# Two chained products behind a convolution: paired 64-row passes, larger units, and a DMA transpose

## The chip, the cores and the metric

One NeuronCore of a Trainium2 chip runs the whole program. The metric is the device time of one execution in microseconds (us), lower is better. The kernel before takes 1038.2 us, the median of 3 runs (1037.63 to 1038.45).

Engines in the text: PE is TensorE (matmuls; PEld is its weight load), DVE is VectorE, ACT is ScalarE, POOL is GpSimd, and SP is SyncE, which here only issues DMAs. Matmuls read SBUF and write PSUM, which has eight banks of 2 KB per partition.

## The reference

Input x has 8 sequences of 4096 tokens with 192 channels. The 192 channels are 8 heads of 24. Each head has 7 weights, put through a softmax; every channel is convolved causally along its sequence with the weights of its head. Then come two products with a product with the cosine between them:

```python
# attention part: x (8, 4096, 192), weight (8, 7)
w = softmax(weight, axis=-1)
x_pad = concatenate([zeros((B, 6, D)), x], axis=1)          # causal
out[b, s, h, g] = sum_k w[h, k] * x_pad[b, s + k, h, g]
# then, on 32768 tokens x 192 channels:
h = x @ w_in            # 192 -> 2048
g = h * np.cos(h)
return g @ w_out        # 2048 -> 192, float32
```

## The kernel before, in words

The tokens are cut into 64 tiles of 512. Constants first: two sets of eight 128x128 band matrices (`band`, lines 93 to 105, and `bandhi`, lines 107 to 121) are put together tap by tap on DVE and POOL from shifted identities and the softmax weights. One matmul with such a matrix convolves 128 tokens; `bandhi` brings in the six tokens that lie across the block's edge. The two weight matrices are loaded in float32 and turned to bf16 on ACT (lines 127 to 133).

For each tile:

- `prep_tile` loads 512 tokens, 128 per block, on SP's queue (line 157), turns them to bf16 on POOL (line 160), and loads the last six tokens of the tile by themselves (`hx`, lines 162 to 166).
- `conv_tile` runs, for each of 4 blocks and 8 heads, two matmuls of 24 columns into `ct_ps` (lines 180 and 182): 64 in a tile. The result, tokens on partitions, goes to `ct_sb` in bf16 (lines 185 and 187). Eight PE transposes (line 191) turn it to channels on partitions, in two halves of 96 channels, and two copies put it into `convT`.
- Product 1 (line 207): for each of 16 blocks of 128 features, two matmuls of 96 rows and 512 columns into one bank, `h_ps` (three buffers).
- ACT computes the cosine as a sine with a shift of pi/2 (line 210), 128x512 at a time, and DVE multiplies `h_ps` by it into `g_sb` (line 211).
- Product 2 (line 224): for each of 4 token blocks, 16 matmuls of 192 columns add up in `o_ps` (one bank), which DVE copies to `o_sb` (line 226). SP stores the tile (line 227).

The order of the instructions on each engine is chosen by the framework's scheduler from the dependencies and the program order. In the trace it mixes the product 2 of a tile with the product 1 of the next, and the convolution of the tile after in small pieces between them.

Of the kernel before, what the change touches and what calls it, by code (L numbers as in the profile page):

```python
# [12 lines left out]
ALU = mybir.AluOpType  # L14


@with_exitstack
def kernel(
# [32 lines left out]
    nc.vector.tensor_reduce(out=wmax, in_=w_sb, axis=mybir.AxisListType.X, op=ALU.max)
# [8 lines left out]
    wsm = consts.tile([H, K], BF16)  # L60
    nc.vector.tensor_scalar(out=wsm, in0=wexp, scalar1=winv, scalar2=None, op0=ALU.mult)
    cidx = consts.tile([H, H * K], FP32)
    nc.gpsimd.iota(cidx, pattern=[[1, H * K]], base=0, channel_multiplier=0, allow_small_or_imprecise_dtypes=True)
    hidx = consts.tile([H, 1], FP32)
    nc.gpsimd.iota(hidx, pattern=[[0, 1]], base=0, channel_multiplier=K, allow_small_or_imprecise_dtypes=True)
    tdiff = consts.tile([H, H * K], FP32)
    nc.vector.tensor_scalar(out=tdiff, in0=cidx, scalar1=hidx, scalar2=None, op0=ALU.subtract)
    ge0 = consts.tile([H, H * K], FP32)
    nc.vector.tensor_scalar(out=ge0, in0=tdiff, scalar1=-0.5, scalar2=None, op0=ALU.is_gt)
    ltK = consts.tile([H, H * K], FP32)  # L70
    nc.vector.tensor_scalar(out=ltK, in0=tdiff, scalar1=float(K) - 0.5, scalar2=None, op0=ALU.is_lt)
    hm = consts.tile([H, H * K], FP32)
    nc.vector.tensor_tensor(out=hm, in0=ge0, in1=ltK, op=ALU.mult)
    wsm_rep = consts.tile([H, H, K], FP32)
    for hh in range(H):
        nc.scalar.copy(wsm_rep[:, hh, :], wsm)
    wsm_exp = consts.tile([H, H * K], BF16)
    nc.vector.tensor_tensor(out=wsm_exp, in0=hm, in1=wsm_rep.rearrange("p a b -> p (a b)"), op=ALU.mult)
    ones8 = consts.tile([H, 128], BF16)
    nc.vector.memset(ones8, 1.0)  # L80
    wb_ps = xtp.tile([128, H * K], FP32)
    nc.tensor.matmul(out=wb_ps, lhsT=ones8, rhs=wsm_exp, start=True, stop=True)
    wb = consts.tile([128, H * K], FP32)
    nc.scalar.copy(wb, wb_ps)
# [4 lines left out]
    identx = consts.tile([128, 128 + K], BF16)  # L89
    nc.vector.memset(identx, 0.0)  # L90
    nc.gpsimd.tensor_copy(out=identx[:, 0:128], in_=ident)

    band = consts.tile([128, H, 128], BF16)
    bacc = consts.tile([128, 2, 128], FP32)
    btmp = consts.tile([128, 2, 128], FP32)
    eng = [nc.vector, nc.gpsimd]
    for h in range(H):
        b = bacc[:, h % 2, :]
        tmp = btmp[:, h % 2, :]
        nc.vector.tensor_scalar(out=b, in0=identx[:, 0:128], scalar1=wb[:, h * K : h * K + 1], scalar2=None, op0=ALU.mult)  # L100
        for k in range(1, K):
            e = eng[k % 2]
            e.tensor_scalar(out=tmp, in0=identx[:, k : k + 128], scalar1=wb[:, h * K + k : h * K + k + 1], scalar2=None, op0=ALU.mult)  # L103
            nc.vector.tensor_tensor(out=b, in0=b, in1=tmp, op=ALU.add)  # L104
        nc.scalar.copy(band[:, h, :], b)  # L105

    bandhi = consts.tile([128, H, 128], BF16)
    dmat = consts.tile([128, 128], FP32)
    nc.gpsimd.iota(dmat, pattern=[[1, 128]], base=0, channel_multiplier=-1, allow_small_or_imprecise_dtypes=True)
    mc = consts.tile([128, K - 1, 128], FP32)  # L110
    for ci in range(K - 1):
        nc.vector.tensor_scalar(out=mc[:, ci, :], in0=dmat, scalar1=float(122 + ci), scalar2=None, op0=ALU.is_equal)
    for h in range(H):
        b = bacc[:, h % 2, :]
        tmp = btmp[:, h % 2, :]
        nc.vector.tensor_scalar(out=b, in0=mc[:, 0, :], scalar1=wb[:, h * K + 6 : h * K + 7], scalar2=None, op0=ALU.mult)
        for ci in range(1, K - 1):
            e = eng[ci % 2]
            e.tensor_scalar(out=tmp, in0=mc[:, ci, :], scalar1=wb[:, h * K + 6 - ci : h * K + 7 - ci], scalar2=None, op0=ALU.mult)  # L119
            nc.vector.tensor_tensor(out=b, in0=b, in1=tmp, op=ALU.add)  # L120
        nc.scalar.copy(bandhi[:, h, :], b)  # L121

    w_in_f32 = consts.tile([HD, 2, Dff], FP32)
    for c in range(2):
        nc.sync.dma_start(out=w_in_f32[:, c, :], in_=moe_w_in[c * HD : (c + 1) * HD, :])
    w_in_sb = consts.tile([HD, 2, Dff], BF16)
    nc.scalar.copy(w_in_sb[:, 0, :], w_in_f32[:, 0, :])
    nc.scalar.copy(w_in_sb[:, 1, :], w_in_f32[:, 1, :])

    w_out_f32 = consts.tile([128, NF, D], FP32)  # L130
    nc.sync.dma_start(out=w_out_f32, in_=moe_w_out.rearrange("(n p) d -> p n d", p=128))
    w_out_sb = consts.tile([128, NF, D], BF16)
    nc.scalar.copy(w_out_sb, w_out_f32)


    xin = ctx.enter_context(tc.tile_pool(name="xin", bufs=3))
    xbf_pool = ctx.enter_context(tc.tile_pool(name="xbf", bufs=2))
    hx_pool = ctx.enter_context(tc.tile_pool(name="hx", bufs=2))
    ct_pool = ctx.enter_context(tc.tile_pool(name="ct", bufs=2))
    convT_pool = ctx.enter_context(tc.tile_pool(name="convT", bufs=2))  # L140
    cos_pool = ctx.enter_context(tc.tile_pool(name="cos", bufs=3))
    gpool = ctx.enter_context(tc.tile_pool(name="g", bufs=2))
    opool = ctx.enter_context(tc.tile_pool(name="o", bufs=3))
    ct_ps_pool = ctx.enter_context(tc.tile_pool(name="ct_ps", bufs=2, space=bass.MemoryType.PSUM))
    h_ps_pool = ctx.enter_context(tc.tile_pool(name="h_ps", bufs=3, space=bass.MemoryType.PSUM))
    o_ps_pool = ctx.enter_context(tc.tile_pool(name="o_ps", bufs=1, space=bass.MemoryType.PSUM))

    def prep_tile(it):
        t0 = it * T
        x_f32 = xin.tile([128, 4, D], FP32)  # L150
        if it % TPB == 0:
            nc.vector.memset(x_f32[0:PAD, 0, :], 0.0)
            nc.sync.dma_start(out=x_f32[PAD:128, 0, :], in_=xf[t0 : t0 + 128 - PAD, :])
            nc.sync.dma_start(out=x_f32[:, 1:4, :],
                              in_=xf[t0 + 128 - PAD : t0 + T - PAD, :].rearrange("(n p) d -> p n d", p=128))
        else:
            nc.sync.dma_start(out=x_f32, in_=xf[t0 - PAD : t0 + T - PAD, :].rearrange("(n p) d -> p n d", p=128))
        x_bf = xbf_pool.tile([128, 4, D], BF16)
        for s in range(4):
            nc.gpsimd.tensor_copy(out=x_bf[:, s, :], in_=x_f32[:, s, :])  # L160
        hx = hx_pool.tile([128, 2, D], FP32)
        nc.sync.dma_start(out=hx[0 : PAD, 0, :], in_=xf[t0 + T - PAD : t0 + T, :])
        nc.gpsimd.memset(hx[:, 1, :], 0.0)
        nc.gpsimd.tensor_copy(out=hx[0:PAD, 1, :], in_=hx[0:PAD, 0, :])  # L164
        hx_bf = hx_pool.tile([128, D], BF16)
        nc.gpsimd.tensor_copy(out=hx_bf, in_=hx[:, 1, :])  # L166
        state["x_bf"] = x_bf
        state["hx_bf"] = hx_bf

    def conv_tile():  # L170
        x_bf = state["x_bf"]
        convT = convT_pool.tile([HD, 2, T], BF16)
        ct_sb = ct_pool.tile([128, 4, D], BF16)
        for sp in range(2):
            ct_ps = ct_ps_pool.tile([128, 2, D], FP32)
            for s2 in range(2):
                s = sp * 2 + s2
                nxt = x_bf[:, s + 1, :] if s < 3 else state["hx_bf"]
                for h in range(H):
                    nc.tensor.matmul(out=ct_ps[:, s2, h * G : (h + 1) * G], lhsT=band[:, h, :],  # L180
# [8 lines left out]
        for c in range(2):  # L189
            for s in range(4):  # L190
                nc.tensor.transpose(ps_t[:, c, s, :], ct_sb[:, s, c * HD : (c + 1) * HD], ident)  # L191
# [66 lines left out]
```

## Time and profile before

| what | value |
|---|---|
| median of 3 runs | 1038.2 us (1037.63 to 1038.45) |
| span of the profiled execution, first to last instruction | 1036.6 us |
| PE busy | 960.7 us (93%) |
| DVE busy | 831.1 us (80%) |
| ACT busy | 724.4 us (70%) |
| POOL busy | 166.8 us (16%) |
| DMA moved | 55.45 MB |

The span is that of one profiled execution; the median of the timed runs lies 1.6 us above it. Busy times overlap across engines, so the engine with the largest busy time isn't by that alone the bound: the chain of work that ended last tells that. A matmul's row lasts from its start to its modelled end, and the next matmul starts before that end, so the time from start to start is what a matmul costs in a row of many. The granted TensorE clock is full speed in this profile.

### The profile page before, as it was taken

The numbers are of one execution on the slowest core, as the hardware profiler recorded it, in microseconds if no ns is written. First come the engines' busy times: TensorE is split into PE (matmuls) and PEld (weight loads), VectorE is DVE, ScalarE is ACT, GpSimd is POOL, SyncE is SP. The second block draws the span as 40 slices with busy tenths as digits, with TensorE's granted clock in tenths as the row PEclk, the third lists the DMA queues.
The fourth block names the chain that finished last, engine by engine and source line by source line (L and its number), as shares of the span: only waits on it lengthen the run. The fifth ranks groups of instructions, "written<-read, shape, count | busy, mean of one in ns | idle before, by whom it ended". The sixth has DMA issues, their size and how long they took to land.

```text
span 1036.6 us, 26549 instructions
## 1 busy us (share of the span) xinstructions
PE 960.7 (93%) x10753; PEld 681.3 (66%) x10753; DVE 831.1 (80%) x1643; ACT 724.4 (70%) x1247; POOL 166.8 (16%) x506
## 2 busy tenths in 40 slices
PE   0039999999999999999999999999999999999997
PEld 0026677777777776777677677767776776777664
DVE  3658888888888888888788888888888888888885
ACT  3028777777777777777777777777677777777874
POOL 4651101110111111111101110111111011111100
PEclk9999999999999999999999999999999999999999
DMA  6001112211221122112111211121112112111010
GB/s 181 17 16 47 54 42 62 63 48 48 62 63 47 48 63 58 52 48 62 51 59 48 62 59 51 48 63 47 52 58 63 48 48 63 58 52 32 32 33 31
DMA packets 70748, 55.45 MB, mean 53 GB/s; under 512 B 2512, under 2 KB 70432, under 8 KB 70432
## 3 DMA queue, kind: packets, MB, share of 16 engines
q1 hardware_dynamic: 70624, 53.75, 17.2%
q8 instruction: 84, 1.38, 0.6%
q14 instruction: 40, 0.33, 0.1%
HBM read 28.57 MB, written 25.17 MB: 52 GB/s over the span
## 4 chain that ended last, share of the span: by engine, by line
PE 91%; POOL 3%; DVE 2%; ACT 1%; DMA 1%; issue 1%; SPq 0%; POOLq 0%
PE h_ps L207 44%; PE o_ps L224 34%; PE ct_ps L182 5%; PE ct_ps L180 5%; PE ps_t L191 4%; POOL btmp L119 1%; POOL btmp L103 1%; DMA w_in_f<-in_moe_w_in_dram 1%; DVE bacc L104 1%; ACT convT L192 0%; DVE bacc L120 0%; ACT cos_sb L210 0%; DVE btmp L103 0%; DVE g_sb L211 0%; DVE btmp L119 0%
## 5 line engine op out<-in xcount | busy, mean ns | idle before, releaser
L210 ACT ACTIVATE cos_sb<-h_ps,halfpi 128x512 bf16<-128x512 f32 x1024 | 660.4, 686 | 243.5 <-PE h_ps L207 222.1
L211 DVE TENSOR_TENSOR g_sb<-h_ps,cos_sb 128x512 bf16<-128x512 f32 x1024 | 667.8, 687 | 141.3 <-ACT cos_sb L210 131.2
L207 PE MATMUL h_ps<-convT,w_in_sb 96*128 96x512 bf16 x2048 | 579.1, 380 | 2.4 <-DVE g_sb L211 0.4
L224 PE MATMUL o_ps<-w_out_sb,g_sb 128*128 128x192 bf16 x4096 | 461.7, 246 | 2.6 <-DVE o_sb L226 1.3
L224 PEld LDWEIGHTS <-g_sb 128*128 128x128 bf16 x4096 | 352.1, 98 | 107.4 <-issue 18.1
L207 PEld LDWEIGHTS <-w_in_sb 96*128 96x128 bf16 x2048 | 185.6, 98 | 63.1 <-issue 5.4
L182 PEld LDWEIGHTS <-bandhi 128*128 128x128 bf16 x2048 | 126.0, 96 | 82.1 <-ACT bandhi L121 47.3
L160 POOL CAST x_bf<-x_f 128x192 bf16<-128x192 f32 x256 | 78.0, 343 | 597.2 <-PE ct_ps L182 597.2
L180 PEld LDWEIGHTS <-band 128*128 128x128 bf16 x2048 | 132.0, 96 | 54.8 <-ACT band L105 19.0
L180 PE MATMUL ct_ps<-x_bf,band 128*128 128x24 bf16 x2048 | 149.5, 174 | 16.2 <-ACT band L105 14.4
L182 PE MATMUL ct_ps<-x_bf,bandhi 128*128 128x24 bf16 x1536 | 116.8, 173 | 45.0 <-ACT bandhi L121 45.0
L226 DVE COPY o_sb<-o_ps 128x192 f32<-128x192 f32 x256 | 90.0, 352 | 24.3 <-PE o_ps L224 22.5
L191 PEld LDWEIGHTS <-ct_sb 128*96 128x96 bf16 x512 | 53.8, 123 | 42.4 <-ACT ct_sb L187 22.9
L191 PE MATMUL ps_t<-ident,ct_sb 128*96 128x128 bf16 x512 | 81.1, 231 | 0.1
L164 POOL COPY hx<-hx 6x192 f32<-6x192 f32 x64 | 21.4, 334 | 180.6 <-DMA hx<-in_x_dram 180.6
L185 DVE CAST ct_sb<-ct_ps 128x192 bf16<-128x192 f32 x128 | 43.5, 348 | 4.5 <-PE ct_ps L182 4.4
L187 ACT CAST ct_sb<-ct_ps 128x192 bf16<-128x192 f32 x128 | 40.5, 318 | 1.4 <-PE ct_ps L182 1.3
L192 ACT COPY convT<-ps_t 96x512 bf16<-96x512 bf16 x64 | 36.5, 570 | 1.0 <-PE ps_t L191 1.0
L182 PE MATMUL ct_ps<-hx_bf,bandhi 128*128 128x24 bf16 x512 | 36.0, 173 | 0.0
L193 DVE COPY convT<-ps_t 96x512 bf16<-96x512 bf16 x64 | 26.2, 410 | 0.0
L104 DVE TENSOR_TENSOR bacc<-bacc,btmp 128x128 f32<-128x128 f32 x48 | 13.4, 300 | 11.8 <-POOL btmp L103 11.6
L166 POOL CAST hx_bf<-hx 128x192 bf16<-128x192 f32 x64 | 22.0, 343 | 0.1
(45 smaller groups left out, 95.1 us busy)
## 6 DMA issues: line engine op xcount, KB each, us to landing
out_dram<-o_sb SPq DMA_DIRECT2D x64, 384.0 KB
x_f<-in_x_dram SPq DMA_DIRECT2D x56, 384.0 KB
x_f<-in_x_dram SPq DMA_DIRECT2D x8, 288.0 KB
w_in_f<-in_moe_w_in_dram SPq DMA_DIRECT2D x2, 768.0 KB
w_out_f<-in_moe_w_out_dram SPq DMA_DIRECT2D x1, 1536.0 KB
hx<-in_x_dram SPq DMA_DIRECT2D x64, 4.5 KB
x_f<-in_x_dram SPq DMA_DIRECT2D x8, 91.5 KB
w_sb<-in_weight_dram SPq DMA_DIRECT2D x1, 0.2 KB
```

What stands on the lines that cost most here:

```text
L160: nc.gpsimd.tensor_copy(out=x_bf[:, s, :], in_=x_f32[:, s, :])
L180: nc.tensor.matmul(out=ct_ps[:, s2, h * G : (h + 1) * G], lhsT=band[:, h, :], rhs=x_bf[:, s, h * G : (h + 1) * G], start=True, stop=False)
L182: nc.tensor.matmul(out=ct_ps[:, s2, h * G : (h + 1) * G], lhsT=bandhi[:, h, :], rhs=nxt[:, h * G : (h + 1) * G], start=False, stop=True)
L185: nc.vector.tensor_copy(out=ct_sb[:, s, :], in_=ct_ps[:, s2, :])
L187: nc.scalar.copy(ct_sb[:, s, :], ct_ps[:, s2, :])
L191: nc.tensor.transpose(ps_t[:, c, s, :], ct_sb[:, s, c * HD : (c + 1) * HD], ident)
L192: nc.scalar.copy(convT[:, 0, :], ps_t[:, 0, :, :])
L207: nc.tensor.matmul(out=h_ps, lhsT=w_in_sb[:, c, f * 128 : (f + 1) * 128], rhs=conv_sb[:, c, :], start=(c == 0), stop=(c == 1))
L210: nc.scalar.activation(out=cos_sb, in_=h_ps, func=AF.Sin, bias=halfpi, scale=1.0)
L211: nc.vector.tensor_tensor(out=g_sb[:, f, :], in0=h_ps, in1=cos_sb, op=ALU.mult)
L224: nc.tensor.matmul(out=o_ps[:, s2, 0:D], lhsT=g_sb[:, f, s * 128 : (s + 1) * 128], rhs=w_out_sb[:, f, :], start=(f == 0), stop=(f == NF - 1))
L226: nc.vector.tensor_copy(out=o_sb[:, s, :], in_=o_ps[:, s2, 0:D])
```

## The change

The kernel is written anew, with the same result. The parts:

- The order on each engine is now that of the program (`manual_schedule`).
- Product 1 splits the 192 channels as 128 + 64 instead of 96 + 96. Two blocks of features (`i` = 0, 1) are handled together: two 64-row matmuls, the first on partitions 0 to 63 and the second on 64 to 127, then two 128-row ones. The last 64 channels therefore stand twice in the transposed data.
- Sine and product take both blocks at once, 128x1024 over two banks; `h` has three buffers of two banks.
- The convolution works on units of 1024 tokens: for each head two matmuls of 8 x 24 = 192 columns; one ACT copy for two heads. The six tokens across an edge come from the block before (`xb[:, 0:UB]`), so no small load is needed.
- The transposes are one crossbar DMA for a unit, on SP's queue, behind a POOL copy that doubles the last 64 channels.
- The output copy is on ACT, two token blocks (one bank) at a time.
- The band matrices come from one row for each head, stored to DRAM, read back with a shift of one element per partition, and reversed on DVE.
- Loads are 1024 tokens, weight casts are on DVE and POOL.

The core of the diff (the lines removed are those of the functions above):

```diff
+    skew = consts.tile([128, H, 256], BF16)
+    nc.scalar.dma_start(out=skew, in_=bass.AP(tensor=rd.tensor, offset=rd.offset, ap=[[1, 128], [LR, H], [1, 256]]))
+    band = consts.tile([128, H, 256], BF16)
+    nc.vector.tensor_copy(out=band, in_=skew[:, :, ::-1])
...
+    def cast_unit(u):
...
+            nc.gpsimd.tensor_copy(out=xb[:, 0, :], in_=bf[u - 1][:, UB, :])
+        nc.gpsimd.tensor_copy(out=xb[:, 1 : UB + 1, :], in_=xt)
...
+    def conv_pair(u, q):
...
+        ps = c_pool.tile([128, 2, UB, G], FP32, name="c_ps")
+        for i in range(2):
+            h = 2 * q + i
+            hs = slice(h * G, (h + 1) * G)
+            nc.tensor.matmul(out=ps[:, i], lhsT=band[:, h, 0:128], rhs=xb[:, 1 : UB + 1, hs], start=True, stop=False)
+            nc.tensor.matmul(out=ps[:, i], lhsT=band[:, h, 128:256], rhs=xb[:, 0:UB, hs], start=False, stop=True)
...
+    def conv_out(q, ct, ps):
+        o = ct[:, :, 2 * q * G : (2 * q + 2) * G].rearrange("p n (i g) -> p i n g", i=2)
+        nc.scalar.copy(o, ps)
...
+    def turn_unit(u):
+        ct = ct_tiles.pop(u)
+        nc.gpsimd.tensor_copy(out=ct[:, :, D:256], in_=ct[:, :, 128:D])
+        t = cT_pool.tile([128, UB, 2, 128], BF16, name="cT")
+        nc.sync.dma_start_transpose(out=t.rearrange("p n c k -> p (n c) k"), in_=ct.rearrange("p n k -> p (n k)"))
...
+    def mm1(t, j):
...
+        h = h_pool.tile([128, 2, T], FP32, name="h")
+        for i in range(2):
+            r = slice(64 * i, 64 * i + 64)
+            nc.tensor.matmul(out=h[:, i, :], lhsT=w2[r, j, :], rhs=c[r, n0 : n0 + NB, 1, :], start=True, stop=False)
+        for i in range(2):
+            f = 2 * j + i
+            nc.tensor.matmul(out=h[:, i, :], lhsT=w1[:, f * 128 : (f + 1) * 128], rhs=x1, start=False, stop=True)
+        cs = cos_pool.tile([128, 2, T], BF16, name="cs")
+        nc.scalar.activation(out=cs, in_=h, func=AF.Sin, bias=halfpi, scale=1.0)
...
+        nc.vector.tensor_tensor(out=g_tiles[t][:, 2 * j : 2 * j + 2, :], in0=h, in1=cs, op=ALU.mult)
...
+    def mm2(t, j):
...
+        s, half = divmod(j, 2)
+        if s % 2 == 0 and half == 0:
+            o_state["ps"] = o_pool.tile([128, 2, 256], FP32, name="o_ps")
...
+        for f in range(half * 8, half * 8 + 8):
+            nc.tensor.matmul(out=ps[:, s % 2, 0:D], lhsT=g[:, f, s * 128 : (s + 1) * 128], rhs=wo[:, f, :],
+                             start=(f == 0), stop=(f == NF - 1))
+        if s % 2 == 1 and half == 1:
+            nc.scalar.copy(sb[:, s - 1 : s + 1, :], ps[:, :, 0:D])
+            if s == NB - 1:
+                nc.sync.dma_start(out=out[t * T : (t + 1) * T, :].rearrange("(n p) d -> p n d", p=128), in_=sb)
...
+    for t in range(NT + 1):
+        u_next = t // TPU + 1
+        for j in range(NP):
+            if t < NT:
+                mm1(t, j)
+                if u_next < NU:
+                    k = (t % TPU) * NP + j
+                    if k < H and k % 2 == 0:
+                        conv_out(k // 2, *conv_pair(u_next, k // 2))
+                    if k == H:
+                        turn_unit(u_next)
+                        if u_next + 1 < NU:
+                            load_unit(u_next + 1)
+                            cast_unit(u_next + 1)
+            if t > 0:
+                mm2(t - 1, j)
```

A tile's 16 blocks are thus 8 pairs `j`, a unit has two tiles and 16 pairs `k`, and at each pair PE does product 1 of tile t, at times a convolution pair, and an eighth of product 2 of tile t - 1.

More of the change, by code (lines that the diff above doesn't have):

```diff
@@ L7 @@
 from concourse import bass_utils, mybir
-from concourse.masks import make_identity
 from concourse._compat import with_exitstack
@@ L14 @@
 ALU = mybir.AluOpType
+PSUM = bass.MemoryType.PSUM
 @with_exitstack
@@ L43 @@
-    pp = xtp
-    ident = consts.tile([128, 128], BF16)
-    make_identity(nc, ident)
-    w_sb = consts.tile([H, K], FP32)
-    nc.sync.dma_start(out=w_sb, in_=weight)
-    wmax = consts.tile([H, 1], FP32)
-    nc.vector.tensor_reduce(out=wmax, in_=w_sb, axis=mybir.AxisListType.X, op=ALU.max)
+    dram = ctx.enter_context(tc.tile_pool(name="dram", bufs=1, space=bass.MemoryType.DRAM))
+    xin = ctx.enter_context(tc.tile_pool(name="xin", bufs=2))
+    xbf_pool = ctx.enter_context(tc.tile_pool(name="xbf", bufs=2))
@@ new lines, with load_unit @@
+    ctx.enter_context(tc.manual_schedule())
+    w_sb = consts.tile([H, K], FP32)
+    nc.scalar.dma_start(out=w_sb, in_=weight)
+    x_tiles = {}
+    def load_unit(u):
+        xt = xin.tile([128, UB, D], FP32, name="x_f")
+        nc.sync.dma_start(out=xt, in_=xf[u * U : (u + 1) * U, :].rearrange("(n p) d -> p n d", p=128))
+        x_tiles[u] = xt
+    load_unit(0)
+    w1_f = consts.tile([128, Dff], FP32)
+    w2_f = consts.tile([128, NP, 128], FP32)
+    w2_src = moe_w_in[128:D, :].rearrange("c (j t f) -> t c j f", t=2, f=128)
@@ L52 @@
+    nc.sync.dma_start(out=w1_f, in_=moe_w_in[0:128, :])
+    for t in range(2):
+        nc.sync.dma_start(out=w2_f[t * 64 : t * 64 + 64, :, :], in_=w2_src[t])
+    wo_f = consts.tile([128, NF, D], FP32)
+    nc.sync.dma_start(out=wo_f, in_=moe_w_out.rearrange("(n p) d -> p n d", p=128))
+    load_unit(1)
+    LR = 512
+    row = consts.tile([H, LR], BF16)
+    nc.vector.memset(row, 0.0)
     negmax = consts.tile([H, 1], FP32)
-    nc.vector.tensor_scalar(out=negmax, in0=wmax, scalar1=-1.0, scalar2=None, op0=ALU.mult)
+    nc.vector.tensor_reduce(out=negmax, in_=w_sb, axis=mybir.AxisListType.X, op=ALU.max)
@@ L59 @@
     nc.vector.reciprocal(winv, wsum)
[L60 to L84, printed above, removed]
+    nc.vector.tensor_scalar(out=row[:, 249 : 249 + K], in0=wexp, scalar1=winv, scalar2=None, op0=ALU.mult)
@@ L90 @@
[L90 to L155, printed above, removed]
-        else:
[L157 to L180, printed above, removed]
-                                     rhs=x_bf[:, s, h * G : (h + 1) * G], start=True, stop=False)
-                    nc.tensor.matmul(out=ct_ps[:, s2, h * G : (h + 1) * G], lhsT=bandhi[:, h, :],
-                                     rhs=nxt[:, h * G : (h + 1) * G], start=False, stop=True)
-                if s2 == 0:
-                    nc.vector.tensor_copy(out=ct_sb[:, s, :], in_=ct_ps[:, s2, :])
-                else:
-                    nc.scalar.copy(ct_sb[:, s, :], ct_ps[:, s2, :])
-        ps_t = xtp.tile([HD, 2, 4, 128], BF16)
-        for c in range(2):
-            for s in range(4):
-                nc.tensor.transpose(ps_t[:, c, s, :], ct_sb[:, s, c * HD : (c + 1) * HD], ident)
-        nc.scalar.copy(convT[:, 0, :], ps_t[:, 0, :, :])
-        nc.vector.tensor_copy(out=convT[:, 1, :], in_=ps_t[:, 1, :, :])
-        return convT
@@ new lines, in conv_unit @@
+    def conv_unit(u):
+        for q in range(H // 2):
+            conv_out(q, *conv_pair(u, q))
+        turn_unit(u)
+    cast_unit(0)
+    nc.gpsimd.tensor_copy(out=w2, in_=w2_f)
+    nc.vector.tensor_copy(out=w1, in_=w1_f)
+    conv_unit(0)
+    cast_unit(1)
+    for q in range(4):
+        nc.vector.tensor_copy(out=wo[:, 4 * q : 4 * q + 4, :], in_=wo_f[:, 4 * q : 4 * q + 4, :])
+    g_tiles = {}
+    o_state = {}
+    def mm1(t, j):
+        c = cT[t // TPU]
+        n0 = (t % TPU) * NB
+        x1 = c[:, n0 : n0 + NB, 0, :]
+        h = h_pool.tile([128, 2, T], FP32, name="h")
[7 more added lines that the diff above has]
+        nc.scalar.activation(out=cs, in_=h, func=AF.Sin, bias=halfpi, scale=1.0)
+        if j == 0:
+            g_tiles[t] = gpool.tile([128, NF, T], BF16, name="g")
+        nc.vector.tensor_tensor(out=g_tiles[t][:, 2 * j : 2 * j + 2, :], in0=h, in1=cs, op=ALU.mult)
```

84 lines of the change are left out of this document (47 added, 37 removed).

## The prediction

> **What bounds the kernel now.** I read the chain that ended last first, then the groups of instructions, then the PE chain of one tile. Engine, busy us and share stand in the first fence; then the chain's shares; then groups with count, busy us, mean ns and idle time before them.
>
> ```profile
> span 1036.6 us, 26549 instructions
> PE 960.7 (93%) x10753; PEld 681.3 (66%) x10753; DVE 831.1 (80%) x1643; ACT 724.4 (70%) x1247; POOL 166.8 (16%) x506
> ...
> PE 91%; POOL 3%; DVE 2%; ACT 1%; DMA 1%; issue 1%; SPq 0%; POOLq 0%
> ...
> L210 ACT ACTIVATE cos_sb<-h_ps,halfpi 128x512 bf16<-128x512 f32 x1024 | 660.4, 686 | 243.5 <-PE h_ps L207 222.1
> L211 DVE TENSOR_TENSOR g_sb<-h_ps,cos_sb 128x512 bf16<-128x512 f32 x1024 | 667.8, 687 | 141.3 <-ACT cos_sb L210 131.2
> L207 PE MATMUL h_ps<-convT,w_in_sb 96*128 96x512 bf16 x2048 | 579.1, 380 | 2.4 <-DVE g_sb L211 0.4
> L224 PE MATMUL o_ps<-w_out_sb,g_sb 128*128 128x192 bf16 x4096 | 461.7, 246 | 2.6 <-DVE o_sb L226 1.3
> ...
> L191 PE MATMUL ps_t<-ident,ct_sb 128*96 128x128 bf16 x512 | 81.1, 231 | 0.1
> ```
>
> PE ends last for 91% of the span, waits 2 to 3 us before its two large groups, and ACT's longest idle (222 us) is a wait for PE. A busy matmul row overlaps the next one, so I take PE's price from the chain, which gives start-to-start time (start, us, what, count), and the convolution's from PE's timeline.
>
> ```profile
> 501.82 0.17 PE ps_t L191 x3
> ...
> 505.42 1.33 PE o_ps L224 x16
> ...
> 511.03 1.08 PE h_ps L207 x5
> ```
>
> ```profile
> 504.95 0.17 PE L180 MATMUL ct_ps<-x_bf,band 128*128 128x24 bf16 x1
> ...
> 505.25 0.17 PE L180 MATMUL ct_ps<-x_bf,band 128*128 128x24 bf16 x1
> ```
>
> A 512-column matmul costs 1.08/5 = 0.216 us, a 192-column one 1.33/16 = 0.083, a 24-column one 0.30/12 = 0.025 (12 steps between those rows), a transpose 0.17/3 = 0.057. The 512-token tile has 32, 64, 64 and 8 of them: 6.91 + 5.31 + 1.60 + 0.46 = 14.3 us, and 64 tiles 914. Two stages (start and end, length, then busy us of PE, PEld, DVE, ACT, POOL) and the first product place them:
>
> ```profile
> 0.00:69.00 69.00, 2.69 (x33) 1.66 (x34) 37.70 (x164) 13.49 (x30) 38.08 (x76) 1.00 0.28 75
> 69.00:1018.00 949.00, 946.46 (x10638) 672.40 (x10637) 784.91 (x1464) 704.60 (x1207) 128.71 (x430) 1.00 0.17 52
> ```
>
> ```profile
> L207 PEld LDWEIGHTS <-w_in_sb x2048: 95/97/158, 72.4 to 1024.3; 96*128 96x128 bf16 x187
> L207 PE MATMUL h_ps<-convT,w_in_sb x2048: 376/377/634, 72.5 to 1024.5; 96*128 96x512 bf16 x187
> ```
>
> So 72.5 us pass before product 1 starts, PE then works without a break, and some 4 us lie behind the last product 2. The runs' median of 1038.2 is 1.6 above this span; I sum against the span and add 1.6.
>
> **The change, part by part.**
>
> *Product 1.* For two blocks of 128 features there were four 96-row matmuls, 4 x 0.216 = 0.864. Now there are two 64-row ones, on different rows of the array and into different banks, and two 128-row ones. If the 64-row ones run side by side, a pair of blocks costs 3 x 0.216 = 0.648, and 512 pairs save 111 us. Call x what the pair loses of that: at best 0, since the rows above show no cost when PE goes between 96 and 128 rows; at worst, if PE empties before and after, twice the tail of a matmul, 2 x (0.377 - 0.216) = 0.32; if they run one after the other, 0.216. Nothing in this trace runs two row halves at once. Nearest is the weight load: two must be ready ahead of the pair where one is hidden now, and one exposed load is 0.097. I take x = 0.10.
>
> The Trainium skill (TensorEngine Tiling (Array Packing), Key Properties) says that changing the tiling mode, not just the tile, drains TensorE, and this kernel changes it twice a pair. No row here shows such a change; by that rule x goes to the emptying end and is the second rival below.
>
> *Convolution.* 64 x 64 = 4096 matmuls of 24 columns (4096 x 0.025 = 102 us) become 32 x 16 = 512 of 192 columns (8 blocks x 24), 512 x 0.083 = 42. Saves 60.
>
> *Transposes.* 512 on PE go: 512 x 0.057 = 29 us saved on PE, and the wait for ct_sb with them. In their place the unit of 1024 tokens has a POOL copy of 512 elements and one 512 KB crossbar DMA on SP, priced under "deadlines".
>
> *PE's sum.* Product 1 332, product 2 4096 x 0.083 = 340, convolution 42: 714 us against 914.
>
> *ACT and DVE, two banks at once.* The sine and product back to back (start, us, engine), and other copies of theirs, by group:
>
> ```profile
> 511.29 1.84 ACT L210 ACTIVATE cos_sb<-h_ps,halfpi 128x512 bf16<-128x512 f32 x3 [1.19 <-PE h_ps L207]
> ...
> 512.01 1.89 DVE L211 TENSOR_TENSOR g_sb<-h_ps,cos_sb 128x512 bf16<-128x512 f32 x3 [0.58 <-ACT cos_sb L210]
> ```
>
> ```profile
> L226 DVE COPY o_sb<-o_ps 128x192 f32<-128x192 f32 x256 | 90.0, 352 | 24.3 <-PE o_ps L224 22.5
> ...
> L187 ACT CAST ct_sb<-ct_ps 128x192 bf16<-128x192 f32 x128 | 40.5, 318 | 1.4 <-PE ct_ps L182 1.3
> ```
>
> ```profile
> 15.15 2.75 ACT L133 CAST w_out_sb<-w_out_f 128x3072 bf16<-128x3072 f32 x1 [2.68 <-DMA w_out_f<-in_moe_w_out_dram]
> ```
>
> ACT: a sine takes 0.686, the next starts (1.84 - 0.686)/2 = 0.577 later, and an element more costs (2.75 - 0.318)/(3072 - 192) = 0.845 ns. 512 elements more are 0.43: 1.12 us long, 1.01 a start, 512 x 1.01 = 517. The 128 convolution and 128 output copies, now all on ACT, have 384 elements, 0.318 + 0.16 = 0.48: 123 more, 640 in all. DVE: a start (1.89 - 0.687)/2 = 0.60, an element (0.687 - 0.352)/320 = 1.05 ns: 1.22 long, 1.13 a start, 579 in all, and no copies any more. At worst two banks cost twice a start, 591 and 614, and ACT 714. PE's 714 + x stays the bound, with ACT 75 us or more behind it when x is added.
>
> *The output bank.* o_ps is still one bank, now emptied on ACT behind a sine. What such a handover costs PE is seen at the end of this trace:
>
> ```profile
> 1026.68 0.37 DVE o_sb L226
> 1027.05 0.04 issue
> 1027.09 1.49 PE o_ps L224 x16
> 1028.59 0.02 issue
> 1028.61 0.37 DVE o_sb L226
> 1028.98 0.04 issue
> 1029.02 1.49 PE o_ps L224 x16
> ...
> 1032.47 0.36 DVE o_sb L226
> ```
>
> Per bank (twice a tile), counted from the start of product 1 of pair 3: product 1 until 0.75, its sine from 0.93 to 2.05, the copy until 2.43, free at 2.48; PE has done eight product-2 matmuls (0.66) and the next product 1 (0.75) by 2.16 and waits 0.32. Where a convolution pair (0.33) lies in between, as for half of the banks, it waits for nothing. 64 x 0.32 = 20 us. Queued behind the waiting product 2 on PE is the next product 1; the three h buffers give 3 x 1.4 = 4.2 us for a chain of 0.93 + 1.12 + 1.22 = 3.3, so ACT and DVE do not run dry.
>
> *Deadlines in a unit.* At the unit's middle SP has in order: the output store (waits for ACT, about 0.7 us into the half), the transpose, the load of the unit after next; POOL then casts that load, and PE needs the transpose and the cast eight pairs later, 8 x 1.41 + 0.3 = 11.6 us on.
>
> ```profile
> q1 hardware_dynamic: 70624, 53.75, 17.2%
> ...
> L160 POOL CAST x_bf<-x_f 128x192 bf16<-128x192 f32 x256 | 78.0, 343 | 597.2 <-PE ct_ps L182 597.2
> ```
>
> ```profile
> 502.23 0.34 SPq L162 DMA_DIRECT2D hx<-in_x_dram  x1
> ...
> 505.13 0.33 POOL L164 COPY hx<-hx 6x192 f32<-6x192 f32 x1 [2.79 <-DMA hx<-in_x_dram]
> ```
>
> A small DMA takes 505.13 - 502.57 = 2.6 us from issue to use. A packet holds a DMA engine for 0.172 x 1036.6 x 16 / 70624 = 40 ns (768 bytes). 512 KB in 256-byte rows is 2048 packets, 2048 x 40 / 16 = 5.2 us, with the round trip 7.8; in bytes at the same rate (53.75 MB in 178 us, 301 GB/s) 1.7, with it 4.3; sixteen 128x128 blocks each with a round trip, 42. No crossbar transfer is in this trace. I take 6 us: a bulk transfer is nearest, in smaller rows. Ready at 0.7 + 6 = 6.7 of 11.6: no stall. The load behind it needs some 5 us (786 KB at 301 GB/s and the round trip) and POOL's cast of 1536 elements 8 x 0.343 = 2.7 at most: ready near 12 with the engines shared, just in time for the convolution behind the first product 1 at 12.4. Each us later would cost 31 us in all. The POOL copy (about 0.7) and the output store (384 KB, 1.3 us on the engines) hide in the same half unit; the 64 small loads of hx and their POOL work go, which nothing on PE's chain waited for.
>
> *Prologue.* Bands were built by DVE and POOL until 69 us. Now softmax, one row stored to DRAM and read back skewed:
>
> ```profile
> 2.10 0.15 DVE L51 TENSOR_REDUCE wmax<-w_sb 8x1 f32<-8x7 f32 x1 [0.75 <-DMA w_sb<-in_weight_dram]
> ...
> 4.15 0.22 DVE L61 TENSOR_SCALAR wsm<-wexp,winv 8x7 bf16<-8x7 f32 x1
> ```
>
> Row ready at 4.4; two DMA round trips to 9.6, and 0.5 MB read beside 4.7 MB of loads (ACT's cast above waited for the first 3.1 MB until 15.15, some 220 GB/s) 3 to 4 more: 13. Reversal on DVE 2 us, four convolution steps of 1.1 (matmuls, tail, ACT copy, one bank), POOL copy, transpose: 13 + 2 + 4.5 + 0.7 + 6 = 26; I take 29, between 25 and 36. The casts of the weights (2.75 us the largest, on ACT) go to DVE and POOL and lie beside the band's reading; uncovered, all three would add some 6 us. The gain is 72.5 - 29 = 43.
>
> *Sum.* 29 until product 1; tile 0 runs without product 2 at ACT's and DVE's pace, 9.4 us, with 6 of PE's 714 in it; the other 708; x: 504 x 0.10 = 50; output bank 20; last copy 0.5; end 4.2: 821 of span, 823 as median.
>
> **Rivals.**
>
> 1. *PE stays the bound.* As summed, 760 to 840: 0.50. For it speaks that PE's starts here are even (0.216, 0.083) whatever lies between them.
> 2. *The halves do not pay.* One after the other: 821 + 504 x 0.116 - 20 (the bank's wait is then covered) = 859, as median 861. Emptying twice: 821 + 504 x 0.22 - 20 = 912, 914. Nothing in the profile speaks against it. 840 to 920: 0.27.
> 3. *A late transfer.* Transpose or load misses its half unit by 1 to 6 us, 31 units: 855 to 1010. For it: everything goes through SP's one queue and 16 shared engines. Against it: q1 used 17.2%. 0.12.
> 4. *Slower, the transpose alone.* If it takes T, a unit is 12.9 (first half) + 0.7 + T, and the whole 29 + 31 units + 39: over 1037 from T = 17.7 us on. At the block-wise end, 42 us, it is some 1,790. Against it: no bulk transfer of this trace moves one block at a time. 0.10.
>
> The Trainium skill (VectorE: DVE Perf Modes, The three transpose paths) gives 1309 ns for a 128x128 block by DMA. Sixteen such in a row would be 21 us, an estimate from that page that lands in rival 4 (about 1,140); this trace has no such transfer to hold it against.
>
> 5. PE's gain is lost one for one and nothing moves: 0.01. It would take the last rival at just its point.
>
> **Numbers.** The likeliest is 823 (alone 760 to 840). At x = 0 the bank waits grow to 0.42 each, 27 us: 778; 760 has half of these covered and the prologue at 25. The range goes to 905, into rival 2 and the first part of 3; about 0.2 is left out. 0.2% (2 us) is about what a measurement of this kernel can tell from no change. Faster: rivals 1 and 2 and nearly all of 3, 0.88; same 0.01; slower 0.11, rival 4 and what of 3 comes near it.
>
> **What would show it.** Two 64-row matmuls starting within some 0.01 us of each other and a pair of 0.65 to 0.75 us; 0.083 us per convolution matmul; sine 1.12 and product 1.22 us long; first product 1 near 29 us; product 2 waiting for ACT's o_sb copy a few tenths, twice a tile; no PE wait on cT. I am wrong if PE's first wait of a unit is for the transpose or for x_bf, if the 64-row matmuls are 0.2 us apart, or if the ACT queue, not PE, ends the chain.

## The result, and the profile after

| | median | runs | span of the profiled execution |
|---|---|---|---|
| before | 1038.2 us | 1037.6 to 1038.5 (3) | 1036.6 us |
| after | 875.0 us | 874.5 to 875.2 (4) | 873.0 us |

The ratio is 0.843 (95% interval 0.842 to 0.844). The prediction was 823 us, 760 to 905. The time lies in that range, 52 us above the likeliest value and outside that value's own range (760 to 840).

The page of the changed kernel: the span, each engine's busy us, share and count, then the chain that ended last by engine and by line, then the costliest groups (busy us, mean ns of one, idle time before them and what ended it).

```profile
span 873.0 us, 15646 instructions
...
PE 835.6 (96%) x6656; PEld 504.3 (58%) x6656; DVE 631.7 (72%) x525; ACT 668.0 (77%) x771; POOL 76.5 (9%) x101
...
PE 84%; ACT 7%; issue 5%; DMA 2%; DVE 0%; POOL 0%; ACTq 0%
PE o_ps L204 35%; PE h L187 27%; PE h L184 16%; ACT o_sb L207 4%; ACT cs L189 3%; PE c_ps L141 3%; PE c_ps L142 2%; DMA skew<-row_d 1%; DMA row_d<-row 1%; DMA cT<-ct 0%; DVE g L192 0%; ACT ct L147 0%; DMA w_sb<-in_weight_dram 0%; ACT L91 0%
```

```profile
L192 DVE TENSOR_TENSOR g<-h,cs 128x1024 bf16<-128x1024 f32 x512 | 626.9, 1225 | 213.5 <-ACT cs L189 213.4
L189 ACT ACTIVATE cs<-h,halfpi 128x1024 bf16<-128x1024 f32 x512 | 570.1, 1114 | 173.5 <-PE h L187 169.0
L204 PE MATMUL o_ps<-wo,g 128*128 128x192 bf16 x4096 | 420.4, 246 | 4.9 <-ACT o_sb L207 1.5
...
L187 PE MATMUL h<-cT,w 128*128 128x512 bf16 x1024 | 310.9, 385 | 0.0
L184 PE MATMUL h<-cT,w 64*128 64x512 bf16 x1024 | 200.5, 388 | 6.4 <-DMA cT<-ct 5.6
L187 PEld LDWEIGHTS <-w 128*128 128x128 bf16 x1024 | 57.9, 97 | 116.5 <-issue 116.5
...
L184 PEld LDWEIGHTS <-w 64*128 64x128 bf16 x1024 | 49.6, 93 | 88.6 <-issue 88.5
```

PE still bounds the kernel: 835.6 of 873.0 us, and ACT's longest idle (169 us) is a wait for PE, as before. ACT's 7% of the chain are the steps in which the chain passes through the output bank's copy and the sine ahead of it. New are the two rows of PEld: PE's weight loads for product 1 stand idle for 116.5 and 88.5 us under "issue", some 0.23 and 0.17 us for each of 512 pairs. They no longer run ahead while the matmul before them works. In the kernel before, product 1's loads had 5.4 us of idle time under "issue" over as many loads:

```profile
L207 PEld LDWEIGHTS <-w_in_sb 96*128 96x128 bf16 x2048 | 185.6, 98 | 63.1 <-issue 5.4
```

One pair shows it (timeline: start, us, engine and line, count, idle time before):

```profile
496.27 0.10 PEld L184 LDWEIGHTS <-w 64*128 64x128 bf16 x2 [0.16 <-issue]
496.27 0.39 PE L184 MATMUL h<-cT,w 64*128 64x512 bf16 x2
496.59 0.11 PEld L187 LDWEIGHTS <-w 128*128 128x128 bf16 x2 [0.23 <-issue]
496.60 0.60 PE L187 MATMUL h<-cT,w 128*128 128x512 bf16 x2
496.82 0.81 PEld L204 LDWEIGHTS <-g 128*128 128x128 bf16 x8
...
497.04 0.82 PE L204 MATMUL o_ps<-wo,g 128*128 128x192 bf16 x8
...
497.79 0.39 PE L184 MATMUL h<-cT,w 64*128 64x512 bf16 x2
```

Two 64-row matmuls take one row of 0.39 us together: they do run side by side. But the 128-row ones start 0.33 us after them, not 0.216, and the next pair's 64-row ones come 0.75 us after the first of eight product-2 matmuls, not 8 x 0.082 = 0.66. The medians of all such steps between 100 and 700 us, worked out from the start times in the trace (a 512-column matmul behind its like takes 216 ns, a 192-column one 82):

```
from               to                 after   zero rows   two pairs   split
64-row             64-row, same pair    3                    4
64-row, pair 1     64-row, pair 2                          223
64-row             128-row            319                  308         319
128-row, product 1 64-row                                  312         322
product 2          64-row             178                              178
128-row            128-row            226       216        225
product 2          128-row                       82         82
```

(after: the changed kernel; the other columns are three of the experiments below; ns.) A change from 64-row to 128-row matmuls costs 319 - 216 = 103 ns, the change back 178 - 82 = 96, and 10 more fall on the second 128-row matmul. The pair loses 0.209 us of what lying side by side would give, and 0.216 is all it could give. Product 1 costs 0.003 + 0.319 + 0.226 + 0.216 + 0.096 = 0.86 us a pair, as the four 96-row matmuls did (0.864).

So the 163 us come from elsewhere: 42 from the start (72.5 to 30.8 us), 57 from the wider convolution matmuls (measured below), 29 from the transposes that left PE (by the prediction's price). The rest, some 35, I did not test. The old order took 960 us from the first product 1 to the last product 2, against 914 by prices, so PE had some 46 us of waits and longer steps there; the new one waits 14 us for the output bank.

### The profile page after: what moved, and what is told of

Same layout as the page of the kernel before. It is cut to its first block, busy times and chain, and to the rows that moved or that the text cites. A ratio compares the mean times of both kernels' runs of the same rounds, so it can differ in the third digit from the quotient of the medians.

```text
span 873.0 us, 15646 instructions
## 1 busy us (share of the span) xinstructions
PE 835.6 (96%) x6656; PEld 504.3 (58%) x6656; DVE 631.7 (72%) x525; ACT 668.0 (77%) x771; POOL 76.5 (9%) x101
## 4 chain that ended last, share of the span: by engine, by line
PE 84%; ACT 7%; issue 5%; DMA 2%; DVE 0%; POOL 0%; ACTq 0%
PE o_ps L204 35%; PE h L187 27%; PE h L184 16%; ACT o_sb L207 4%; ACT cs L189 3%; PE c_ps L141 3%; PE c_ps L142 2%; DMA skew<-row_d 1%; DMA row_d<-row 1%; DMA cT<-ct 0%; DVE g L192 0%; ACT ct L147 0%; DMA w_sb<-in_weight_dram 0%; ACT L91 0%; DVE band L105 0%
## 5 line engine op out<-in xcount | busy, mean ns | idle before, releaser
L192 DVE TENSOR_TENSOR g<-h,cs 128x1024 bf16<-128x1024 f32 x512 | 626.9, 1225 | 213.5 <-ACT cs L189 213.4
L189 ACT ACTIVATE cs<-h,halfpi 128x1024 bf16<-128x1024 f32 x512 | 570.1, 1114 | 173.5 <-PE h L187 169.0
L204 PE MATMUL o_ps<-wo,g 128*128 128x192 bf16 x4096 | 420.4, 246 | 4.9 <-ACT o_sb L207 1.5
L204 PEld LDWEIGHTS <-g 128*128 128x128 bf16 x4096 | 351.4, 98 | 106.7 <-issue 23.5
L187 PE MATMUL h<-cT,w 128*128 128x512 bf16 x1024 | 310.9, 385 | 0.0
L184 PE MATMUL h<-cT,w 64*128 64x512 bf16 x1024 | 200.5, 388 | 6.4 <-DMA cT<-ct 5.6
L187 PEld LDWEIGHTS <-w 128*128 128x128 bf16 x1024 | 57.9, 97 | 116.5 <-issue 116.5
L184 PEld LDWEIGHTS <-w 64*128 64x128 bf16 x1024 | 49.6, 93 | 88.6 <-issue 88.5
L147 ACT CAST ct<-c_ps 128x384 bf16<-128x384 f32 x128 | 60.4, 472 | 20.1 <-PE c_ps L142 20.1
L141 PE MATMUL c_ps<-x_bf,band 128*128 128x192 bf16 x256 | 53.8, 250 | 22.0 <-DVE halfpi L108 20.3
L207 ACT COPY o_sb<-o_ps 128x384 f32<-128x384 f32 x128 | 60.4, 472 | 5.8 <-PE o_ps L204 5.8
L142 PE MATMUL c_ps<-x_bf,band 128*128 128x192 bf16 x256 | 54.0, 251 | 0.0
L141 PEld LDWEIGHTS <-band 128*128 128x128 bf16 x256 | 25.6, 100 | 35.4 <-DVE halfpi L108 20.3
L142 PEld LDWEIGHTS <-band 128*128 128x128 bf16 x256 | 25.4, 99 | 17.3 <-issue 2.9
```

The source lines that it names most:

```text
L141: nc.tensor.matmul(out=ps[:, i], lhsT=band[:, h, 0:128], rhs=xb[:, 1 : UB + 1, hs], start=True, stop=False)
L142: nc.tensor.matmul(out=ps[:, i], lhsT=band[:, h, 128:256], rhs=xb[:, 0:UB, hs], start=False, stop=True)
L147: nc.scalar.copy(o, ps)
L184: nc.tensor.matmul(out=h[:, i, :], lhsT=w2[r, j, :], rhs=c[r, n0 : n0 + NB, 1, :], start=True, stop=False)
L187: nc.tensor.matmul(out=h[:, i, :], lhsT=w1[:, f * 128 : (f + 1) * 128], rhs=x1, start=False, stop=True)
L189: nc.scalar.activation(out=cs, in_=h, func=AF.Sin, bias=halfpi, scale=1.0)
```

## The experiments

Each kernel ran beside the kernel before on the same chip; there the kernel before took 1037.5 to 1038.1 us. The first theory, "change": PE pays some 0.1 us for each change between 64-row and 128-row matmuls. Its rivals: the cost lies in the 64-row pair itself, or in the written-out order.

**No 64-row matmuls at all.** The weights of the last 64 channels stand among rows of zeros, so that both blocks run as 128-row passes; all else stays.

```diff
-            r = slice(64 * i, 64 * i + 64)
-            nc.tensor.matmul(out=h[:, i, :], lhsT=w2[r, j, :], rhs=c[r, n0 : n0 + NB, 1, :], start=True, stop=False)
+            nc.tensor.matmul(out=h[:, i, :], lhsT=w2[:, 2 * j + i, :], rhs=c[:, n0 : n0 + NB, 1, :], start=True, stop=False)
```

> The last 64 channels are taken in 128-row passes too, with zeros in the weight rows of the other half: four full passes for a pair of feature blocks, and no 64-row matmul anywhere. Theory 'change' (every step between 64-row and 128-row work costs some 0.10 us, 0.21 a pair with what follows it): a pair costs 4 x 0.216 + 0.66 = 1.52 us, as it does now (0.43 + 0.21 + 0.216 + 0.66), so the time stays within 8 us of 875. Rival 'order' (PE loses 0.2 us at that place of the program whatever the rows, at its wait for an h buffer): 0.216 more for each of 512 pairs, some 980.

Measured: 876.5 us (876.0 to 876.7), ratio 0.844 (0.843 to 0.846). Its timeline:

```profile
501.78 0.58 PE L206 MATMUL o_ps<-wo,g 128*128 128x192 bf16 x5
502.19 0.59 PE L186 MATMUL h<-cT,w 128*128 128x512 bf16 x2
502.62 0.59 PE L189 MATMUL h<-cT,w 128*128 128x512 bf16 x2
```

Four passes follow each other at 216 ns (column "zero rows"), and product 2 at 82 on both sides. Twice the passes on half-empty rows cost what the pairing costs, to 1.5 us in 875. Here the pairing gains next to nothing, and the order is not what was lost.

**Two pairs for each change.** 128-row matmuls of pair 1, 64-row ones of pairs 1 and 2, 128-row ones of pair 2, then two eighths of product 2: two changes for two pairs instead of four.

```diff
+        wide(0, True)
+        narrow(0, False)
+        narrow(1, True)
+        wide(1, False)
...
-        for j in range(NP):
+        for j in range(0, NP, 2):
```

> Two pairs together: 128-row passes of the first, 64-row of the first, 64-row of the second, 128-row of the second, then both eighths of product 2. Half as many changes between 64 and 128 rows, the same matmuls. Theory 'change': 256 x 0.2 = 52 us less, and the waits for the output bank (13 us) mostly covered: 812 to 823. Rival 'pair' (each 64-row pair loses 0.2 us of itself, since its weight loads are not pulled ahead): only the bank waits go, some 862; its two 64-row pairs would stand 0.32 apart and not 0.216.

Measured: 807.4 us (807.2 to 807.5), ratio 0.778 (0.777 to 0.779). Its page and timeline:

```profile
PE 771.3 (96%) x6656; PEld 491.8 (61%) x6656; DVE 608.0 (75%) x525; ACT 645.4 (80%) x771; POOL 76.4 (9%) x101
...
PE 95%; DMA 3%; ACT 1%; DVE 0%; issue 0%; POOL 0%; ACTq 0%
```

```profile
503.04 0.59 PE L185 MATMUL h<-cT,w 128*128 128x512 bf16 x2
...
503.57 0.60 PE L190 MATMUL h<-cT,w 64*128 64x512 bf16 x4
...
504.11 0.60 PE L185 MATMUL h<-cT,w 128*128 128x512 bf16 x2
504.55 1.48 PE L214 MATMUL o_ps<-wo,g 128*128 128x192 bf16 x16
...
505.87 0.38 PE L185 MATMUL h<-cT,w 128*128 128x512 bf16 x1
```

Four 64-row matmuls take 0.60 us, the length of two 128-row ones: the pairs follow each other at 223 ns, so nothing is lost in the pair itself. The two changes stand before and behind them (312 and 308 ns, 96 and 92 over 216). Two pairs with product 2 take 505.87 - 503.04 = 2.83 us instead of 3.04; 256 times 0.21 is 54 us, and the waits for the output bank (14 us) go. That makes 68 us, and the time fell by 67.6. The theory "change" holds, and "pair" (862 us) falls.

**Four changes a pair.** A 128-row matmul between the two 64-row ones.

```diff
         for i in range(2):
             r = slice(64 * i, 64 * i + 64)
             nc.tensor.matmul(out=h[:, i, :], lhsT=w2[r, j, :], ...
-        for i in range(2):
             f = 2 * j + i
             nc.tensor.matmul(out=h[:, i, :], lhsT=w1[:, f * 128 : (f + 1) * 128], ...
```

> A 128-row matmul stands between the two 64-row ones of a pair, so that they cannot run side by side and four changes are made for a pair in place of two. Theory 'change': 4 x 0.216 + 4 x 0.10 + 0.66 = 1.92 us a pair against 1.52, 512 x 0.42 = 215 more less 13 of covered bank waits: about 1075. Rival 'pair' (0.2 us for the two 64-row matmuls, not for changes): 110 more, about 975.

Measured: 1090.3 us (1083.9 to 1096.6), ratio 1.048 (1.042 to 1.054), slower than the kernel before. Its timeline:

```profile
501.83 0.39 PE L184 MATMUL h<-cT,w 64*128 64x512 bf16 x1
502.15 0.39 PE L186 MATMUL h<-cT,w 128*128 128x512 bf16 x1
...
502.47 0.39 PE L184 MATMUL h<-cT,w 64*128 64x512 bf16 x1
...
502.79 0.39 PE L186 MATMUL h<-cT,w 128*128 128x512 bf16 x1
```

Within product 1 each matmul now starts 0.32 us behind the one before. The nearer theory by far is "change" (1075 against 975). The trace has what lies above it, for the profiled execution (1096.6 us, the longest of the four). In every kernel here PE's first steps are longer than the later ones, in the changed kernel until 35.9 us. In this run that lasts until 83.9 us: a step from 64-row to 128-row takes 0.539 us there and 0.319 later, one of product 2 takes 0.160 and later 0.082. Summed over the steps from the first product 1 on, that costs 22.7 us, against 2.2 in the changed kernel; with 2.2 the run would have taken 1076. Why the slow stretch lasted so long here isn't known, and the two runs near 1084 us have no profile. The mean granted clock of this profile, 1.000, doesn't show the stretch: the trace's first record of the clock begins at its end, at 83.9 us. (In the kernel before, too, the steps are long until 80.2 us, where its first record begins.)

**Convolution back to 24 columns.**

```diff
-            nc.tensor.matmul(out=ps[:, i], lhsT=band[:, h, 0:128], rhs=xb[:, 1 : UB + 1, hs], start=True, stop=False)
-            nc.tensor.matmul(out=ps[:, i], lhsT=band[:, h, 128:256], rhs=xb[:, 0:UB, hs], start=False, stop=True)
+            for n in range(UB):
+                nc.tensor.matmul(out=ps[:, i, n], lhsT=band[:, h, 0:128], rhs=xb[:, n + 1, hs], start=True, stop=False)
+                nc.tensor.matmul(out=ps[:, i, n], lhsT=band[:, h, 128:256], rhs=xb[:, n, hs], start=False, stop=True)
```

> The changed kernel with its convolution matmuls cut back to 24 columns (4096 instead of 512), all else as it is. Theory 'PE bound': a 24-column matmul was 0.025 us and a 192-column one is 0.082, so PE gets 4096 x 0.025 - 512 x 0.082 = 60 us more, and the time rises from 875 to about 930 (some 5 us less where the added work covers waits for the output bank). Rival 'hidden': the convolution lies beside ACT's and DVE's work, and the time stays within 10 us of 875.

Measured: 932.4 us (931.8 to 933.1), ratio 0.899 (0.897 to 0.900). The wide convolution is worth 57.4 us, and the price of start-to-start steps carried over (60 expected).

**One bank at a time, in the same tiles.** Sine and product for each block by itself, `h` and `cs` still tiles of two banks.

```diff
-        nc.scalar.activation(out=cs, in_=h, func=AF.Sin, bias=halfpi, scale=1.0)
-        nc.vector.tensor_tensor(out=g_tiles[t][:, 2 * j : 2 * j + 2, :], in0=h, in1=cs, op=ALU.mult)
+        for i in range(2):
+            nc.scalar.activation(out=cs[:, i, :], in_=h[:, i, :], func=AF.Sin, bias=halfpi, scale=1.0)
+            nc.vector.tensor_tensor(out=g_tiles[t][:, 2 * j + i, :], in0=h[:, i, :], in1=cs[:, i, :], op=ALU.mult)
```

> Sine and product over one bank at a time, as before the change; nothing else. ACT needs 2 x 0.577 in place of 1.01 us a pair and stays below PE's 1.52. Theory 'PE': within 3 us of 875, or up to 10 more where the copy of the output bank stands behind a longer sine (0.15 for 64 banks). Rival 'ACT sets the pace': 0.14 x 512 = 74 more.

Measured: 1245.1 us (1242.8 to 1246.7), ratio 1.199 (1.198 to 1.201). Both theories missed it by far. Its waits (engine and line, what was waited for, us in all, times, longest) and its timeline:

```profile
DVE g L193 <- ACT cs L192: 514.3, 822, 9.9
ACT cs L192 <- DVE g L193: 391.7, 512, 0.8
...
PE o_ps L205 <- ACT o_sb L208: 251.5, 127, 3.2
```

```profile
502.58 0.69 ACT L192 ACTIVATE cs<-h,halfpi 128x512 bf16<-128x512 f32 x1 [1.06 <-PE h L187]
503.30 0.69 DVE L193 TENSOR_TENSOR g<-h,cs 128x512 bf16<-128x512 f32 x1 [1.06 <-ACT cs L192]
...
504.02 0.69 ACT L192 ACTIVATE cs<-h,halfpi 128x512 bf16<-128x512 f32 x1 [0.76 <-DVE g L193]
```

The second sine of a pair waits for the first product, once in each of the 512 pairs: ACT and DVE take turns on one tile. The new theory: the order is kept by tile, and the short instructions themselves cost little. The next kernel tests it.

**One bank at a time, each bank a tile of its own.**

```diff
-        h = h_pool.tile([128, 2, T], FP32, name="h")
+        hs = [h_pool.tile([128, T], FP32, name="h") for _ in range(2)]
...
+        for i in range(2):
+            cs = cos_pool.tile([128, T], BF16, name="cs")
+            nc.scalar.activation(out=cs, in_=hs[i], func=AF.Sin, bias=halfpi, scale=1.0)
+            nc.vector.tensor_tensor(out=g_tiles[t][:, 2 * j + i, :], in0=hs[i], in1=cs, op=ALU.mult)
```

> Sine and product over one bank at a time again, but each bank is a tile of its own (six h tiles of one bank, six sine tiles), so nothing orders the second sine behind the first product. Theory 'tile': the 1245 us of the kernel that cut sine and product inside the shared two-bank tile came from that order, not from the shorter instructions; here ACT needs 1024 x 0.686 + 121 = 823 us beside PE's 836, so PE still ends the chain and the time is 875 to 895. Rival 'instructions': one-bank sines and products cost that much in themselves, and the time is above 1000.

Measured: 870.2 us (869.6 to 870.3), ratio 0.838 (0.837 to 0.840). Its groups:

```profile
L193 DVE TENSOR_TENSOR g<-h,cs 128x512 bf16<-128x512 f32 x1024 | 659.4, 686 | 175.8 <-ACT cs L192 175.7
L192 ACT ACTIVATE cs<-h,halfpi 128x512 bf16<-128x512 f32 x1024 | 649.2, 688 | 104.3 <-PE h L187 104.3
```

With the same lengths of sine and product the waits of ACT for DVE are gone, and the time is 375 us shorter: it was the shared tile. (`h` and `cs` were split together; which of the two set the order isn't shown.) It is even 4.8 us below the changed kernel, which I had not expected (875 to 895). The copy of the output bank now waits behind a sine of 0.69 us and not of 1.11, and the disturbed step from product 1 to product 2 (the 90th percentile of it) is 366 ns instead of 432: 64 x 0.066 = 4.2 us. So the two-bank form is not what made the kernel faster.

**Two pairs, and the skewed read ahead of the loads.** The row store and the skewed read stand on SP's queue before the loads of the weights and of unit 1; the casts of w_out go to POOL.

```diff
     nc.sync.dma_start(out=skew, ...)
+    nc.sync.dma_start(out=w1_f, in_=moe_w_in[0:128, :])
+    for t in range(2):
+        nc.sync.dma_start(out=w2_f[t * 64 : t * 64 + 64, :, :], in_=w2_src[t])
+    load_unit(1)
+    nc.sync.dma_start(out=wo_f, in_=moe_w_out.rearrange("(n p) d -> p n d", p=128))
```

> The kernel with two pairs per change of mode (807.4 us), with the row store and the skewed read put on SP's queue ahead of the loads of w_in, w_out and unit 1, and the casts of w_out on POOL. Theory 'loads ahead': the skewed read landed at 19.9 us because its row store waited six microseconds and the read nine behind 4.7 MB of loads; alone they land near 11, product 1 starts near 25 instead of 31, and the time is 800 to 803. Rival 'round trips': the two transfers cost that in themselves, and the time stays within 2 us of 807.

Measured: 800.9 us (800.4 to 802.1), ratio 0.772 (0.771 to 0.773): 6.5 us below the two-pair kernel, the fastest of all with the next one. Its timeline:

```profile
10.17 0.69 DVE L104 COPY band<-skew 128x2048 bf16<-128x2048 bf16 x1 [5.78 <-DMA skew<-row_d]
...
17.44 5.03 SPq L154 DMA_TRANSPOSE cT<-ct  x1
...
24.46 1.01 PE L184 MATMUL h<-cT,w 128*128 128x512 bf16 x2 [8.62 <-DMA cT<-ct]
```

The band is there at 10.17 us instead of 19.87, but product 1 starts only 6.7 us sooner: the first transpose now runs beside the loads of w_out and takes 7.0 us from issue to use (17.44 to 24.46), 4.4 in the two-pair kernel.

**The same with banks of their own.** The own-tile edit shown above, made on the 800.9 us kernel.

> The 800.9 us kernel (two pairs per change, skewed read ahead of the loads) with sine and product one bank at a time, each bank a tile of its own. A pair of one-bank sines took 1.26 us where the two-bank sine takes 1.11, so ACT needs 512 x 1.26 + 121 = 766 us beside PE's 771. Theory 'only PE counts': ACT still fits beside PE and the sines start 0.2 us earlier; the time is 796 to 805. Rival 'two banks pay here': with ACT and PE level, each waits for the other at the turns, and the time is 812 to 840.

Measured: 801.1 us (800.9 to 802.7), ratio 0.772 (0.771 to 0.773): no difference. ACT's busy time goes from 644.9 to 717.1 us and the time does not move; only PE counts.

## Why the prediction was right and wrong

**The bound: right.** PE stayed the bound with ACT behind it, and the kernels that changed PE's work moved by about that amount. The time lay in the range only because the range reached into rival 2; the reasons given for 823 us lead to 760 to 840.

**The term that failed: x, in "product 1".** I put what a pair loses at 0.10 us and reckoned it as one exposed weight load (0.097) a pair. It measured 0.209. The size of the row fitted, but the reason and the count were wrong. I had expected the second load of the pair to be exposed; the two 64-row matmuls start 3 ns apart, so it costs next to nothing. The cost falls on the changes, and the pair changes twice, into the 64-row matmuls and out of them. Each change costs about as much as one weight load takes (0.103 and 0.096 us, against 0.093 to 0.098 for a load). 504 x 0.109 = 55 us. The first sign I named (64-row matmuls 0.01 us apart) was seen at 0.003; the second (a pair of 0.65 to 0.75) failed at 0.76 with the change back counted to product 2, at 0.86 with both.

The rule I weighed, that changing the tiling mode drains TensorE (the Trainium skill, TensorEngine Tiling (Array Packing), Key Properties), agrees with the runs: the cost follows the number of changes through zero, one, two and four of them a pair. It states no price; here it was 0.09 to 0.11 us, less than the 0.16 by which I bounded an emptying. With it the result is what rival 2 (840 to 920) described, between its two points of 861 and 914, and I gave that too little. Nothing here settles whether the 0.1 us is the array running empty or the weight load that isn't issued ahead: at a change the timeline has the load and its own matmul starting within 5 ns of each other (496.59 and 496.60), where elsewhere the load starts with the matmul before. The slow stretch at the start doesn't settle it either. A 512-column step doubles there (0.216 to 0.427 us), while a change behind one goes from 0.103 to 0.112 only and its load from 0.096 to 0.105, as if the load set the cost; but a change behind product 2 goes from 0.096 to 0.140, with its load at 0.102.

**The rest of the sum,** each against what the trace of the changed kernel has. The start (timeline), and where product 2 begins and ends (its line: ns of one, first and last start):

```profile
19.57 0.69 DVE L105 COPY band<-skew 128x2048 bf16<-128x2048 bf16 x1 [15.21 <-DMA skew<-row_d]
...
26.46 1.86 SPq L155 DMA_TRANSPOSE cT<-ct  x1
...
30.84 0.61 PE L184 MATMUL h<-cT,w 64*128 64x512 bf16 x2 [5.60 <-DMA cT<-ct]
```

```profile
L204 PE MATMUL o_ps<-wo,g x4096: 242/246/246, 43.1 to 868.7; 128*128 128x192 bf16 x196
```

Tile 0 lasts from 30.84 to 43.06 less the first product 1 of tile 1 (0.8); the output bank's waits are the 65 steps from product 1 to product 2 that exceed 0.216 us, by 0.216 in the median.

| term | predicted | measured |
|---|---|---|
| start of product 1 | 29 | 30.8 |
| tile 0 | 9.4 | 11.4 |
| x | 504 x 0.10 = 50 | 504 x 0.209 = 105 |
| output bank | 64 x 0.32 = 20 | 65 x 0.216 = 14 |
| last copy and what follows | 0.5 + 4.2 = 4.7 | 4.3 |

The differences add up to 821 + 1.8 + 2.0 + 55 - 6 - 0.4 = 873, and the span was 873.0. PE's slow start costs 2.2 us and lies in tile 0, which may be what that term left out; no kernel here separates it from the pace of ACT and DVE. The convolution matmul (0.082 against 0.083), the sine and the product (1.114 and 1.225 us against 1.12 and 1.22) were right.

*The start* came out near for the wrong reasons: the skewed read landed at 19.6 and not 13 us (it stood behind the loads, as the kernel with the read ahead showed), while the reversal took 0.7 and not 2 us and the transpose 4.4 and not 6. *The output bank* was waited for as described, one disturbed bank in two, with 0.22 us instead of 0.32, since the slower pair covered more. The unit's middle and such a wait in the changed kernel:

```profile
511.60 0.60 PE L187 MATMUL h<-cT,w 128*128 128x512 bf16 x2
511.73 0.47 ACT L207 COPY o_sb<-o_ps 128x384 f32<-128x384 f32 x1
...
512.25 0.82 PE L204 MATMUL o_ps<-wo,g 128*128 128x192 bf16 x8
...
512.70 3.17 SPq L155 DMA_TRANSPOSE cT<-ct  x1
...
515.93 0.57 SPq L69 DMA_DIRECT2D x_f<-in_x_dram  x1
...
521.08 1.46 POOL L125 CAST x_bf<-x_f 128x1536 bf16<-128x1536 f32 x1 [9.85 <-DMA x_f<-in_x_dram]
...
524.62 0.25 PE L141 MATMUL c_ps<-x_bf,band 128*128 128x192 bf16 x1
```

Product 2 starts 0.65 us after the 128-row matmuls instead of 0.44, at the end of ACT's copy. *The deadlines* held: the cast ends at 522.5 and is needed at 524.6. Rivals 3 and 4 fell with the transfer's rows (issue to landing, us; then PE's waits for it: us, times, longest):

```profile
cT<-ct SPq DMA_TRANSPOSE x32, 5.0
```

```profile
PE h L184 <- DMA cT<-ct: 5.6, 1, 5.6
```

A transpose takes 5.0 us (6 taken), and PE waited for one once, the first. The 21 us estimated from the block price of the Trainium skill (VectorE: DVE Perf Modes, The three transpose paths, 1309 ns for a 128x128 block) are not borne out: sixteen blocks in one transfer took 5.0 us.

**Where I overrated a part:** "sine and product over two banks" was costed rightly and put off the path rightly; the runs add that it pays nothing at all here, with 801.1 against 800.9 us in the fastest form.

## What to carry to other kernels

Before packing narrow matmuls side by side, count the changes of row mode that the order makes and price each at a measured step: here at 0.1 us a change, one 512-column pair gains 0.216 and two changes eat it all, so group the narrow ones until each change serves several. When a price is taken from a near row, check how often per loop it falls due; the size taken here fitted and the count was half. Two engines that work on halves of one tile may be made to take turns; give each half a tile of its own before blaming the instruction size.

## What was not expected of the hardware

The price of a change hardly depends on its direction or on the matmul before it: 96 ns behind 192 columns, 92 to 106 behind 512. Not every difference in rows is such a change: in the kernel before, where 96-row and 128-row matmuls take turns, the median step between them is 83 ns behind 192 columns and 215 behind 512, about as among their like (82 and 216). And when ACT and DVE took turns and PE idled, PE's clock fell as well: the mean granted clock of that kernel was 0.91 in its profile, full speed in the others, and the same 6656 matmuls took 945 us of busy time instead of 836.

```profile
core 0: 1241.0 us, clock 0.910
```
